# Small tensors of a router moved to PSUM, additions and factors moved to ScalarE, and the last expert's matmuls put in another order

## The chip, the cores and the metric

The kernel runs on one core of one Trainium2 chip. The metric is the device time of one execution in microseconds (us); a smaller one is better. Shown are the median of three runs and one profiled execution.

## The reference

Three stages follow each other. First windowed attention with four sink keys over 4 batches, 8 heads, 768 positions and 64 values per head; then a SoLU layer on 3072 tokens; then a mixture of eight experts, of which each token takes the one with the largest logit.

```python
scores = np.where(is_sink | in_window, q @ k.T / 8, -1e9)
a = np.exp(scores - max); a = a / (sum(a) + 1e-9)          # attention
x = concat_heads(a @ v)                                     # 3072 x 512
h = x @ w_in; e = np.exp(h - max)                           # SoLU layer, 512 -> 1024
solu = h * e / (sum(e) + 1e-9)
ln = (solu - mean) / sqrt(var + 1e-6) * g_ln
x = ln @ w_out                                              # 3072 x 512
logits = x @ w_gate; idx = argmax(logits); gate = softmax(logits)[idx]
out[idx == e] = gate * (relu(x[idx == e] @ w1[e]) @ w2[e])  # eight experts
```

## The kernel before

The attention (a_... functions) goes through 32 units n of two heads and 384 query rows. For one unit, a_scores computes six blocks of scores; each block is masked and scaled on VectorE (L246, L247), exponentiated on ScalarE with its sum (L250), and after the six blocks 1e-9 is added to the six sums (L256), the reciprocal taken (L257), and GpSimd scales the probabilities (L259 pk, L268 psk). a_sinks(u) transposes the sink probabilities of two units on TensorE (L285); a_trans and a_out transpose the others (L299), mask them on GpSimd (L303, L305) and multiply by the values (L315, L321). The first NATP = 5 units multiply fp32 operands directly (L238); later ones use operands split into a high and a low part of type fp32r (L241, L242). a_scores takes a generator mid, which is a_sinks for a pair of units; it is run after the fourth of the six score blocks.

At the same time the weights w_in and w_out are decoded from eight-byte words and split (decode, load_w_in, load_w_out: L367, L368, L369, L381, L382, L416, L417). load_w_out first makes two factors of 128 x 8 from g_ln (g_s L388, g_l L389).

The second stage (m_... functions) takes 24 tiles of 128 tokens: m_in (x by w_in, L472 to L474), m_act (exponential, moments and normalisation; small 128 x 1 columns of the tile sc are combined on VectorE, L487 to L505), m_tr (transposes, L521), m_out (by w_out together with eight logit columns, L543 to L545; then the router on tiles of 128 x 8, L551 to L559), and m_route, which ranks the tile's tokens within their experts by two small matmuls (L570, L571) from the one-hot tile oh and the running count acc, and stores their ids through GpSimd (L579).

The third stage sorts the experts by their counts and runs each with a fixed capacity; f_in is the first matmul of an expert (L868 to L870), f_out the second (L938 to L940). The eighth has one block of 128 rows; for it f_in_rows keeps tokens on the rows (L894 to L896), transposes the result back (L904), and f_out multiplies 512 columns at a time, evicts them (L945) and stores them by an indirect DMA of GpSimd (L946). G.drain() (L1025) is traced between the two for the last expert, behind the last GpSimd split of its weights (L784).

Attention and second stage are interleaved by estimated costs that the generators yield. Over this order the framework places each engine's instructions in a queue of its own with the aid of a planner that simulates times; issue_after(i) says that an instruction comes after i on its engine. Each engine then works through its queue in order, and semaphores join the engines. PSUM has eight banks: three go round under the tag psa, five under psm; the function ps chooses by name.

```python
ATT, MOE, flip = ("s", "tp", "skp", "av", "le"), ("h", "lt", "x2", "wt", "wt2", "rk", "dt", "dh"), [0]
```

Of the kernel before, what the change touches and what calls it, by code (L numbers as in the profile page):

```python
# [8 lines left out]
F32 = mybir.dt.float32  # L9
# [47 lines left out]
def body(ctx, tc, a):  # L57
# [133 lines left out]
    copied = []  # L191
# [31 lines left out]
    def a_scores(n, mid=()):  # L223
# [5 lines left out]
        for i in range(3):  # L229
            for r in range(2):  # L230
# [4 lines left out]
                if n < NATP:  # L235
                    q, k = qk_t[n][r]
                    with tc.issue_after(par_m.ins) if n == 0 else ExitStack():
                        T.matmul(s[:, 0:272], q[rows, qs], k[rows, ks], start=True, stop=True)  # L238
                else:
                    q, ql, k = qk_t[n][r]  # L240
                    T.matmul(s[:, 0:272], q[:, qs], k[:, ks], start=True, stop=False)  # L241
                    T.matmul(s[:, 0:272], ql[:, qs], k[:, ks], start=False, stop=True)  # L242
# [10 lines left out]
            if i == 1:  # L253
                yield from mid
        P = P.rearrange("p r i c -> p (r i) c")
        V.tensor_scalar(out=sm, in0=sm, scalar1=1.0e-9, scalar2=None, op0=ALU.add)  # L256
# [14 lines left out]
    def a_sinks(u):  # L271
# [12 lines left out]
        for i in range(3):  # L284
            T.transpose(t[:, 128 * i:128 * i + 128], psk[:, i].rearrange("p a b c -> p (a b c)"), ident)  # L285
# [99 lines left out]
    def load_w_out(flush=False):  # L385
        sc = SC_OUT * (1.0 if flush else RAW)
        with tc.issue_after(vx[0].ins) if pin[0] else ExitStack():
            V.tensor_scalar(out=g_s, in0=g_sb, scalar1=sc, scalar2=None, op0=ALU.mult)  # L388
            V.tensor_scalar(out=g_l, in0=g_sb, scalar1=1.0 / SC_OUT, scalar2=None, op0=ALU.mult)  # L389
# [45 lines left out]
    acc = const.tile([128, NE], BF16, name="acc")  # L435
    V.memset(acc, 0.0)
    iot8 = const.tile([128, NE], F32, name="iot8")
# [44 lines left out]
    def m_act(t):  # L482
# [10 lines left out]
        V.scalar_tensor_tensor(out=sm, in0=sm, scalar=1.0e-9, in1=sc[:, 3:4], op0=ALU.add, op1=ALU.add)  # L493
        V.scalar_tensor_tensor(out=es, in0=sm, scalar=1.0e-6, in1=sm, op0=ALU.mult, op1=ALU.mult)
# [38 lines left out]
    def m_out(t, row0, mid=()):  # L533
        lh, ll = ln_t.pop(t)
        xr = xrow[t % NXR]
        L = const.tile([128, NE], F32, tag="L", name="L", bufs=2)
        q = const.tile([128, 4], F32, tag="q", name="q", bufs=2)
        oh = const.tile([128, NE], BF16, tag="oh", name="oh", bufs=3)
        for c in range(2):
# [9 lines left out]
            if c == 0:  # L549
                lg = p[:, 256:264]  # L550
# [6 lines left out]
                V.tensor_scalar(out=oh, in0=iot8, scalar1=q[:, 2:3], scalar2=None, op0=ALU.is_equal)  # L557
# [9 lines left out]
    def m_route(t, ids, free=False):  # L567
# [3 lines left out]
        T.matmul(p[:, 0:NE], ones_b, acc, start=False, stop=True)  # L571
        r = const.tile([128, NE], F32, tag="r", name="r")
        s_ = const.tile([128, 1], F32, tag="s_", name="s_", bufs=3)
        si = const.tile([128, 1], I32, tag="si", name="si", bufs=3)
        V.tensor_tensor(out=acc, in0=acc, in1=oh, op=ALU.add)
        V.tensor_tensor(out=r, in0=p[:, 0:NE], in1=rowb, op=ALU.add)  # L576
# [98 lines left out]
    def count():  # L675
        p = ps("ct")
        T.matmul(p[:, 0:NE], ones_b, acc, start=True, stop=True)
        V.tensor_copy(cnt, p[:, 0:NE])

    def plan_head():  # L680

        count()
# [164 lines left out]
    def f_in(r):  # L847
# [5 lines left out]
        if ROOM[r] == 128:  # L853
            yield from f_in_rows(r)
# [601 lines left out]
```

## Time and profile before

| | |
|---|---|
| median of 3 runs | 808.34 us (807.8 to 811.78) |
| profiled execution | 805.58 us, its span 803.6 us |
| TensorE (PE) busy | 774.0 us, 96% of the span, 5005 matmuls |
| VectorE (DVE) busy | 471.9 us, 59%, 1760 instructions |
| ScalarE (ACT) busy | 459.1 us, 57% |
| GpSimd (POOL) busy | 357.9 us, 45% |
| mean granted TensorE clock | 0.983 of full speed |

The span is from the first to the last instruction. Engines work side by side, so the busy shares don't add up; a share over the whole span is a mean over stages with different limits. A busy TensorE isn't one at its peak, because matmuls are pipelined and their ends are modelled.

### The profile page before, as it was taken

How to read it: one execution, taken by the hardware profiler on the slowest of the kernel's cores; microseconds unless marked ns; L12 is line 12 of the kernel's file. 1: busy time of each engine (PE TensorE's matmuls, PEld its weight loads, DVE VectorE, ACT ScalarE, POOL GpSimd, SP SyncE). 2: the span in 40 equal slices, each digit the busy share in tenths (PEclk: the TensorE clock that was granted, in tenths of full speed). 3: DMA queues.
4: the chain of work that ended last, by engine and by line, in shares of the span. 5: the costliest groups of instructions: out<-in, count | busy, mean ns of one | idle time of the engine just before them, and what ended most of it. 6: DMA issues, size and time to landing. Idle time of an engine off the chain costs nothing.

```text
span 803.6 us, 15251 instructions
## 1 busy us (share of the span) xinstructions
PE 774.0 (96%) x5005; PEld 667.1 (83%) x5005; DVE 471.9 (59%) x1760; ACT 459.1 (57%) x1209; POOL 357.9 (45%) x396
## 2 busy tenths in 40 slices
PE   6799999999999999999999999999999999999996
PEld 3487788888888977988888889898978888989885
DVE  6788747668657666667486566436324444545541
ACT  5776857758758657667576464154414343536442
POOL 4955264553635545445623021445326244535543
PEclk9869999999999999999999999999999999999999
DMA  9696354596555855458720271484375517663640
GB/s 333 182 277 161 99 139 140 109 144 141 129 121 136 180 103 146 125 129 115 149 68 14 23 256 42 137 290 150 117 257 184 182 59 214 220 207 101 227 174 29
DMA packets 64218, 120.81 MB, mean 150 GB/s; under 512 B 11068, under 2 KB 32190, under 8 KB 64130
## 3 DMA queue, kind: packets, MB, share of 16 engines
q1 hardware_dynamic: 56594, 97.06, 45.8%
q0 software_dynamic: 5088, 13.88, 4.9%
q10 hardware_dynamic: 2448, 8.80, 3.2%
q8 instruction: 42, 0.69, 0.4%
q14 instruction: 46, 0.38, 0.3%
HBM read 80.61 MB, written 13.28 MB: 117 GB/s over the span
## 4 chain that ended last, share of the span: by engine, by line
PE 79%; DVE 10%; ACT 3%; DMA 3%; issue 3%; POOL 1%; POOLq 0%; SPq 0%; ACTq 0%; DVEq 0%
PE ht L868 6%; PE ht L870 6%; PE ht L869 6%; PE y L938 5%; PE y L940 5%; PE x L543 5%; PE y L939 5%; PE x L545 5%; PE h L472 5%; PE x L544 5%; PE h L473 5%; PE av L321 4%; PE h L474 4%; PE s L241 3%; PE lt L521 2%
## 5 line engine op out<-in xcount | busy, mean ns | idle before, releaser
L543 PE MATMUL x<-woh,lh 128*128 128x256 f32 (+1 forms) x384 | 111.5, 291 | 0.7 <-DVE r L576 0.7
L545 PE MATMUL x<-woh,ll 128*128 128x256 f32 (+1 forms) x384 | 109.6, 286 | 0.0
L544 PE MATMUL x<-wol,lh 128*128 128x256 f32 (+1 forms) x384 | 108.8, 284 | 0.0
L250 ACT ACTIVATE P<-P,mx 128x144 f32<-128x144 f32 x192 | 78.3, 409 | 46.3 <-DVE mx L247 43.7
L776 ACT ACTIVATE wh<-wst 128x1024 fp32r<-128x1024 f32 x64 | 67.4, 1058 | 47.4 <-PE ht L869 27.9
L784 POOL TENSOR_TENSOR wl<-wst,wh 128x1024 fp32r<-128x1024 f32 x28 | 67.7, 2419 | 56.9 <-ACT wh L776 49.7
L204 POOL TENSOR_TENSOR d<-d,A 128x560 fp32r<-128x560 f32 (+1 forms) x27 | 33.8, 1253 | 108.1 <-ACT A L203 98.4
L869 PE MATMUL ht<-xel,wh 128*128 128x288 f32 (+5 forms) x256 | 81.2, 319 | 0.0
L870 PE MATMUL ht<-xeh,wl 128*128 128x288 f32 (+5 forms) x256 | 81.1, 318 | 0.0
L784 DVE TENSOR_TENSOR wl<-wst,wh 128x1024 fp32r<-128x1024 f32 x36 | 54.6, 1524 | 44.8 <-ACT wh L776 44.8
L868 PE MATMUL ht<-xeh,wh 128*128 128x288 f32 (+5 forms) x256 | 79.9, 318 | 0.0
L938 PE MATMUL y<-wh,hh 128*128 128x512 f32 x192 | 77.9, 406 | 1.2 <-DVE hl L877 1.2
L472 PE MATMUL h<-wih,bxh 128*128 128x512 f32 x192 | 78.4, 408 | 0.2
L473 PE MATMUL h<-wil,bxh 128*128 128x512 f32 x192 | 76.3, 397 | 0.0
L940 PE MATMUL y<-wh,hl 128*128 128x512 f32 x192 | 76.0, 397 | 0.0
L939 PE MATMUL y<-wl,hh 128*128 128x512 f32 x192 | 75.8, 395 | 0.0
L474 PE MATMUL h<-wih,bxl 128*128 128x512 f32 x192 | 74.1, 397 | 0.0
L543 PEld LDWEIGHTS x<-woh,lh 128*128 128x128 f32 x384 | 72.3, 188 | 2.2 <-ACT bxh L831 0.9
L545 PEld LDWEIGHTS x<-woh,ll 128*128 128x128 f32 x384 | 72.3, 188 | 1.2 <-issue 0.7
L544 PEld LDWEIGHTS x<-wol,lh 128*128 128x128 f32 x384 | 72.4, 189 | 0.6
L247 DVE CUSTOM_DVE_ANT_0 P<-s,mk 128x144 f32<-128x144 f32 x192 | 55.7, 300 | 20.8 <-PE s L242 11.3
L246 DVE COPY_PREDICATED s<-pick,s 128x128 f32<-128x128 int32 x160 | 44.9, 291 | 38.4 <-PE s L242 34.8
(279 smaller groups left out, 2014.8 us busy)
## 6 DMA issues: line engine op xcount, KB each, us to landing
wst<-w SPq DMA_DIRECT2D x64, 512.0 KB, 4.3
d<-qk SPq DMA_DIRECT2D x15, 472.0 KB, 3.7
x_d<-xrow SPq DMA_DIRECT2D x24, 264.0 KB, 6.4
d<-qk SPq DMA_DIRECT2D x13, 400.0 KB, 3.6
B<-A SPq DMA_DIRECT2D x27, 192.0 KB, 4.0
A<-A SPq DMA_DIRECT2D x27, 192.0 KB, 2.7
B<-A SPq DMA_DIRECT2D x15, 332.0 KB, 5.0
w<-w_in ACTq DMA_DIRECT2D x8, 512.0 KB, 6.6
```

The source lines that it names most:

```text
L472: T.matmul(h, xh[k], wih[:, k, cs], start=(k == 0), stop=False)
L473: T.matmul(h, xh[k], wil[:, k, cs], start=False, stop=False)
L543: T.matmul(p[:, 0:n], lh[:, k, :], woh[:, k, c, 0:n], start=(k == 0), stop=False)
L544: T.matmul(p[:, 0:n], lh[:, k, :], wol[:, k, c, 0:n], start=False, stop=False)
L545: mm = T.matmul(p[:, 0:n], ll[:, k, :], woh[:, k, c, 0:n], start=False, stop=(k == 7))
L784: return (G if c % 2 and r else V).tensor_tensor(out=l_, in0=st_w.pop((r, which, c)), in1=raw(h_), op=ALU.subtract)
L868: T.matmul(o, wh[:, k, fs], xh(k), start=(k == 0), stop=False)
L869: T.matmul(o, wh[:, k, fs], xl(k), start=False, stop=False)
L870: T.matmul(o, wl[:, k, fs], xh(k), start=False, stop=(k == 3))
L938: T.matmul(o, hh[:, k, sl], wh, start=(k == 0), stop=False)
L939: T.matmul(o, hh[:, k, sl], wl, start=False, stop=False)
L940: T.matmul(o, hl[:, k, sl], wh, start=False, stop=(k == 7))
```

## The change

Six places. (1) In a_scores the 1e-9 is added by ScalarE. (2) The factors g_s and g_l are made by ScalarE, placed behind an exponential (pin) in place of a VectorE instruction (vx). (3) In m_act two columns are combined by tensor_scalar with a per-partition operand in place of scalar_tensor_tensor. (4) In m_out the tile L lies in the PSUM bank that holds the logits; oh is compared from L; the running count is a new tile for each token tile (accs), written in m_out; in m_route the tile r lies in PSUM, and the addition to acc is left out there. (5) For the first eight units the sinks' generator runs after all six score blocks, and the first three pairs' transposes are placed behind the latest score matmul. (6) The last expert is one function, f_rows, which takes the 512 output columns in two halves, transposes the first half of the hidden values before the last quarter of them is computed, begins the second matmul with three of its eight row blocks between the two transposes' turns, evicts the two halves one after the other, and issues the store; f_out isn't called for it, and G.drain() is traced behind it.

```diff
@@ -188,7 +188,7 @@
-    copied = []
+    copied, last_s = [], [None]
@@ -235,11 +235,11 @@
                     with tc.issue_after(par_m.ins) if n == 0 else ExitStack():
-                        T.matmul(s[:, 0:272], q[rows, qs], k[rows, ks], start=True, stop=True)
+                        last_s[0] = T.matmul(s[:, 0:272], q[rows, qs], k[rows, ks], start=True, stop=True)
                 else:
...
                     T.matmul(s[:, 0:272], q[:, qs], k[:, ks], start=True, stop=False)
-                    T.matmul(s[:, 0:272], ql[:, qs], k[:, ks], start=False, stop=True)
+                    last_s[0] = T.matmul(s[:, 0:272], ql[:, qs], k[:, ks], start=False, stop=True)
                 cc = slice(3 * r + i, 3 * r + i + 1)
@@ -250,10 +250,10 @@
                 yield 0.45 if n < NATP else 0.23
-            if i == 1:
+            if i == (2 if n < 8 else 1):
                 yield from mid
         P = P.rearrange("p r i c -> p (r i) c")
-        V.tensor_scalar(out=sm, in0=sm, scalar1=1.0e-9, scalar2=None, op0=ALU.add)
+        A.activation(out=sm, in_=sm, func=AF.Copy, bias=1.0e-9)
         V.reciprocal(sm, sm)
@@ -281,8 +281,9 @@
         t = ps("skp")
-        for i in range(3):
-            T.transpose(t[:, 128 * i:128 * i + 128], psk[:, i].rearrange("p a b c -> p (a b c)"), ident)
+        with tc.issue_after(last_s[0].ins) if u < 3 else ExitStack():
+            for i in range(3):
+                T.transpose(t[:, 128 * i:128 * i + 128], psk[:, i].rearrange("p a b c -> p (a b c)"), ident)
         A.activation(out=skt, in_=t[:, 0:384], func=AF.Copy, scale=odd)
@@ -384,9 +385,9 @@
         sc = SC_OUT * (1.0 if flush else RAW)
-        with tc.issue_after(vx[0].ins) if pin[0] else ExitStack():
-            V.tensor_scalar(out=g_s, in0=g_sb, scalar1=sc, scalar2=None, op0=ALU.mult)
-            V.tensor_scalar(out=g_l, in0=g_sb, scalar1=1.0 / SC_OUT, scalar2=None, op0=ALU.mult)
+        with tc.issue_after(pin[0].ins) if pin[0] else ExitStack():
+            A.activation(out=g_s, in_=g_sb, func=AF.Copy, scale=sc)
+            A.activation(out=g_l, in_=g_sb, func=AF.Copy, scale=1.0 / SC_OUT)
@@ -432,8 +433,9 @@
     V.memset(ones_b, 1.0)
-    acc = const.tile([128, NE], BF16, name="acc")
+    acc = const.tile([128, NE], BF16, name="acc0")
     V.memset(acc, 0.0)
+    accs, looped = {0: acc}, [False]
     iot8 = const.tile([128, NE], F32, name="iot8")
@@ -490,8 +492,8 @@
                                    accum_out=sc[:, 4 + c:5 + c])
-        V.scalar_tensor_tensor(out=sm, in0=sm, scalar=1.0e-9, in1=sc[:, 3:4], op0=ALU.add, op1=ALU.add)
-        V.scalar_tensor_tensor(out=es, in0=sm, scalar=1.0e-6, in1=sm, op0=ALU.mult, op1=ALU.mult)
+        V.tensor_scalar(out=sm, in0=sm, scalar1=1.0e-9, scalar2=sc[:, 3:4], op0=ALU.add, op1=ALU.add)
+        V.tensor_scalar(out=es, in0=sm, scalar1=1.0e-6, scalar2=sm, op0=ALU.mult, op1=ALU.mult)
         V.tensor_scalar(out=mu, in0=mu, scalar1=sc[:, 5:6], scalar2=-1.0 / (32 * DF), op0=ALU.add, op1=ALU.mult)
@@ -533,7 +535,6 @@
         xr = xrow[t % NXR]
-        L = const.tile([128, NE], F32, tag="L", name="L", bufs=2)
         q = const.tile([128, 4], F32, tag="q", name="q", bufs=2)
@@ -547,14 +548,18 @@
             if c == 0:
-                lg = p[:, 256:264]
+                lg, L = p[:, 256:264], p[:, 272:272 + NE]
                 V.tensor_reduce(out=q[:, 0:1], in_=lg, axis=AX.X, op=ALU.max)
...
                 V.tensor_reduce(out=q[:, 2:3], in_=L, axis=AX.X, op=ALU.min)
-                V.tensor_scalar(out=oh, in0=iot8, scalar1=q[:, 2:3], scalar2=None, op0=ALU.is_equal)
+                V.tensor_scalar(out=oh, in0=L, scalar1=q[:, 2:3], scalar2=None, op0=ALU.is_equal)
+                if not looped[0]:
+                    accs[t + 1] = const.tile([128, NE], BF16, tag="acc", name="acc", bufs=4)
+                    V.scalar_tensor_tensor(out=accs[t + 1], in0=L, scalar=q[:, 2:3], in1=accs[t], op0=ALU.is_equal,
+                                           op1=ALU.add)
                 V.tensor_scalar(out=q[:, 1:2], in0=q[:, 1:2], scalar1=1.0e-9, scalar2=None, op0=ALU.add)
@@ -568,12 +573,13 @@
         T.matmul(p[:, 0:NE], tri, oh, start=True, stop=False)
-        T.matmul(p[:, 0:NE], ones_b, acc, start=False, stop=True)
-        r = const.tile([128, NE], F32, tag="r", name="r")
+        T.matmul(p[:, 0:NE], ones_b, acc if looped[0] else accs[t], start=False, stop=True)
+        r = p[:, 0:NE]
         s_ = const.tile([128, 1], F32, tag="s_", name="s_", bufs=3)
         si = const.tile([128, 1], I32, tag="si", name="si", bufs=3)
-        V.tensor_tensor(out=acc, in0=acc, in1=oh, op=ALU.add)
-        V.tensor_tensor(out=r, in0=p[:, 0:NE], in1=rowb, op=ALU.add)
+        if looped[0]:
+            V.tensor_tensor(out=acc, in0=acc, in1=oh, op=ALU.add)
+        V.tensor_tensor(out=r, in0=r, in1=rowb, op=ALU.add)
         V.scalar_tensor_tensor(out=r, in0=r, scalar=1.0, in1=oh, op0=ALU.mult, op1=ALU.mult, accum_out=s_)
@@ -672,14 +678,14 @@
-    def count():
+    def count(n=NT):
         p = ps("ct")
-        T.matmul(p[:, 0:NE], ones_b, acc, start=True, stop=True)
+        T.matmul(p[:, 0:NE], ones_b, acc if looped[0] else accs[n], start=True, stop=True)
         V.tensor_copy(cnt, p[:, 0:NE])
...
-        count()
+        count(TE + 1)
         V.scalar_tensor_tensor(out=lead, in0=cnt, scalar=float(NE), in1=e8, op0=ALU.mult, op1=ALU.subtract)
@@ -851,7 +857,7 @@
         if ROOM[r] == 128:
-            yield from f_in_rows(r)
+            yield from f_rows(r)
             return
@@ -879,34 +885,65 @@
-    def f_in_rows(r):
+    def f_rows(r):
         hp = pool2["h"]
...
+        w1, w2 = wt[r]
         hh, hl = ht_t[r]
         (xh, xl, c0, n), = xe_t.pop(r)
...
+        p = [ps("ht") for _ in range(2)]
+        hr = [hp.tile([128, DM], F32, tag="y", name="hr", bufs=3) for _ in range(2)]
+        ys = [ps("y") for _ in range(2)]
+        y = hp.tile([128, DM], F32, tag="y", name="y", bufs=3)
+        j = first[r]
+
+        def rows(c):
+            wh, wl = w1[c]
+            o = p[c // 2][:, 256 * (c % 2):256 * (c % 2) + 256]
+            for k in range(4):
+                T.matmul(o, xh(k), wh[:, k, :], start=(k == 0), stop=False)
+                T.matmul(o, xh(k), wl[:, k, :], start=False, stop=False)
+                T.matmul(o, xl(k), wh[:, k, :], start=False, stop=(k == 3))
+
+        def turn(c):
             t = ps("xt")
             for k in range(4):
...
+                i = T.transpose(t[:, 128 * k:128 * k + 128], hr[c][:, 128 * k:128 * k + 128], ident)
             tv = t.rearrange("p (k n) -> p k n", k=4)
...
             V.tensor_tensor(out=hl[:, sl, 0:128], in0=tv, in1=raw(hh)[:, sl, 0:128], op=ALU.subtract)
...
+            return i
+
+        def columns(d, *ks):
+            ds, o = slice(256 * d, 256 * d + 256), ys[d][:, 0:256]
+            for x, w in ((hh, 0), (hh, 1), (hl, 0)):
+                for k in ks:
+                    i = T.matmul(o, x[:, k, 0:128], w2[k // 2][w][:, k % 2, ds], start=(x is hh and k + w == 0),
+                                 stop=(x is hl and k == 7))
+            return i
+
+        rows(0)
+        yield
+        rows(1)
+        yield
+        A.activation(out=hr[0], in_=p[0], func=AF.Relu)
+        rows(2)
+        yield
+        with tc.issue_after(turn(0).ins):
+            rows(3)
+        yield
+        A.activation(out=hr[1], in_=p[1], func=AF.Relu)
+        with tc.issue_after(columns(0, 0, 1, 2).ins):
+            i = turn(1)
+        with tc.issue_after(i.ins):
+            columns(0, 3)
+            columns(1, 0, 1, 2, 3)
+        for d in range(2):
+            columns(d, 4, 5, 6, 7)
+            A.activation(out=y[:, 256 * d:256 * d + 256], in_=ys[d][:, 0:256], func=AF.Copy, scale=gate[:, j:j + 1])
+        G.indirect_dma_start(out=a["out"], out_offset=bass.IndirectOffsetOnAxis(ap=dst[:, j:j + 1], axis=0), in_=y,
+                             in_offset=None, bounds_check=B * S - 1, oob_is_err=False)
+        yield
@@ -1028,7 +1065,7 @@
                 next(nx, None)
-            for m, _ in enumerate(f_out(r, m0)):
+            for m, _ in enumerate(f_out(r, m0) if more else ()):
                 for _ in range((4 * m + 4) // nm - 4 * m // nm):
@@ -1177,7 +1214,7 @@
             open_moe1(c2, "_g")
-            dec_p[0] = mp
+            dec_p[0], looped[0] = mp, True
             for g in (load_w_in(True), load_w_out(True)):
```

## Rows read from the trace of the kernel before

**Rows 1.** Windows: us, busy (count) of PE, PEld, DVE, ACT, POOL; PE clock; DMA.

```profile
40.00:56.00 16.00, 15.02 (x67) 12.55 (x67) 14.06 (x49) 11.30 (x31) 7.60 (x11) 0.50 0.88 246
56.00:290.00 234.00, 232.28 (x1637) 200.69 (x1637) 161.47 (x701) 164.17 (x491) 118.56 (x139) 1.00 0.61 140
290.00:304.00 14.00, 11.51 (x78) 9.52 (x78) 11.12 (x37) 8.96 (x30) 3.75 (x4) 1.00 0.49 122
304.00:520.00 216.00, 212.42 (x1474) 188.45 (x1474) 138.25 (x630) 128.73 (x375) 78.78 (x95) 1.00 0.45 106
```

**Rows 2.** Timeline of VectorE around 303 us, and TensorE just after it.

```profile
302.05 0.84 DVE L493 SCALAR_TENSOR_TENSOR sc<-sc 128x1 f32<-128x1 f32 x1
...
304.01 0.17 PE L570 MATMUL rk<-oh,tri 128*128 128x8 bf16 x1 [1.21 <-DVE L L552]
```

**Rows 3.** VectorE's groups by shape: busy us, mean ns; idle before, releaser.

```profile
L557 DVE TENSOR_SCALAR oh<-iot,q 128x8 bf16<-128x8 f32 x24 | 10.4, 434 | 0.0
L555 DVE SCALAR_TENSOR_TENSOR L<-L,iot 128x8 f32<-128x8 f32 x24 | 9.5, 395 | 2.1 <-ACT ex L554 2.0
L256 DVE TENSOR_SCALAR sm<-sm 128x6 f32<-128x6 f32 x32 | 8.9, 279 | 8.5 <-ACT P L250 8.4
L493 DVE SCALAR_TENSOR_TENSOR sc<-sc 128x1 f32<-128x1 f32 x24 | 8.7, 362 | 0.0
L494 DVE SCALAR_TENSOR_TENSOR sc<-sc 128x1 f32<-128x1 f32 x24 | 7.4, 308 | 0.0
L575 DVE TENSOR_TENSOR acc<-acc,oh 128x8 bf16<-128x8 bf16 x24 | 6.7, 281 | 10.0 <-PE rk L571 9.6
L552 DVE TENSOR_SCALAR L<-x,q 128x8 f32<-128x8 f32 x24 | 5.3, 221 | 0.1
...
L685 DVE TENSOR_SCALAR lead<-lead,led 128x8 f32<-128x8 f32 x1 | 0.2, 221 | 0.0
```

**Rows 4.** Single lines: duration in ns, minimum/median/maximum, first and last start.

```profile
L493 DVE SCALAR_TENSOR_TENSOR sc<-sc x24: 146/156/1201, 76.4 to 478.0; 128x1 f32<-128x1 f32 x24
L495 DVE TENSOR_SCALAR sc<-sc x24: 198/202/215, 76.6 to 479.5; 128x1 f32<-128x1 f32 x24
```

**Rows 5.** ScalarE's groups by shape, same columns as rows 3.

```profile
L500 ACT ACTIVATE sc<-sc 128x1 f32<-128x1 f32 x24 | 4.7, 199 | 1.2 <-DVE sc L499 1.2
L926 ACT ACTIVATE y<-y,gate 128x256 f32<-128x256 f32 x2 | 1.0, 476 | 5.7 <-PE y L923 5.7
```

**Rows 6.** Timelines of VectorE and GpSimd near 38 us.

```profile
37.98 2.37 DVE L388 TENSOR_SCALAR g_s<-gw_sb 128x8 f32<-128x8 f32 x1
39.47 0.85 POOL L305 TENSOR_SCALAR_AFFINE_SELECT pt<-pt 128x768 f32<-128x768 f32 x1
```

**Rows 7.** Timeline of TensorE, early: start, us, group [idle before, releaser].

```profile
24.60 0.55 PE L285 MATMUL skp<-ident,psk 128*128 128x128 f32 x3 [2.70 <-POOL psk L268]
...
40.37 2.40 PE L321 MATMUL wt<-pt,vd 128*64 128x256 f32 x12 [1.47 <-POOL pt L305]
43.38 1.09 PE L395 MATMUL wt<-ident,dec 128*128 128x128 f32 x4 [0.61 <-DVE dec L369]
```

**Rows 8.** Timeline of the last expert: TensorE, then ScalarE's last eviction.

```profile
783.66 0.36 PE L894 MATMUL ht<-wh,xeh 128*128 128x256 f32 x1
...
789.07 0.28 PE L896 MATMUL ht<-wh,xel 128*128 128x256 f32 x1
...
790.09 0.66 PE L904 MATMUL xt<-ident,hr 128*128 128x128 f32 x4 [0.30 <-ACT hr L899]
790.57 0.50 PE L938 MATMUL y<-wh,hh 128*128 128x512 f32 x1
...
796.30 0.39 PE L940 MATMUL y<-wh,hl 128*128 128x512 f32 x1
...
796.78 0.69 ACT L945 ACTIVATE y<-y,gate 128x512 f32<-128x512 f32 x1 [5.40 <-PE y L940]
```

**Rows 9.** GpSimd's drain, in the columns of rows 4.

```profile
L1025 POOLq DRAIN  x1: 10020/10020/10020, 785.5 to 785.5; - x1
```

More of the change, by code (lines that the diff above doesn't have):

```diff
@@ L880, in f_in @@
         xe_t.pop(r)
-    def f_in_rows(r):
+    def f_rows(r):
         hp = pool2["h"]
-        w1 = wt[r][0]
+        w1, w2 = wt[r]
         hh, hl = ht_t[r]
         (xh, xl, c0, n), = xe_t.pop(r)
-        hr = []
-        for c in range(2):
-            p = ps("ht")
-            for q in range(2):
-                wh, wl = w1[2 * c + q]
-                o = p[:, 256 * q:256 * q + 256]
-                for k in range(4):
-                    T.matmul(o, xh(k), wh[:, k, :], start=(k == 0), stop=False)
-                    T.matmul(o, xh(k), wl[:, k, :], start=False, stop=False)
-                    T.matmul(o, xl(k), wh[:, k, :], start=False, stop=(k == 3))
-                yield
-            h_ = hp.tile([128, DM], F32, tag="y", name="hr", bufs=3)
-            A.activation(out=h_, in_=p, func=AF.Relu)
-            hr.append(h_)
-        for c in range(2):
+        p = [ps("ht") for _ in range(2)]
[11 more added lines that the diff above has]
+        def turn(c):
             t = ps("xt")
             for k in range(4):
-                T.transpose(t[:, 128 * k:128 * k + 128], hr[c][:, 128 * k:128 * k + 128], ident)
+                i = T.transpose(t[:, 128 * k:128 * k + 128], hr[c][:, 128 * k:128 * k + 128], ident)
             tv = t.rearrange("p (k n) -> p k n", k=4)
@@ L908, in f_in_rows @@
             V.tensor_tensor(out=hl[:, sl, 0:128], in0=tv, in1=raw(hh)[:, sl, 0:128], op=ALU.subtract)
-            yield
+            return i
[28 more added lines that the diff above has]
+        yield
     def f_out(r, m0=0, m1=None, late=()):
```

## The prediction

> **What bounds the kernel now.** I read the windows first, then VectorE's groups and the spread of single lines in them, and last the timelines of the two ends with the waits of TensorE. The windows settle most of it: from 56 to 290 us TensorE is busy 232.28 of 234 us, and from 304 to 520 us 212.42 of 216 [rows 1]. The clock is granted at 1.00 in all three of the windows after 56 us, and the diff touches nothing of the expert stage behind 520 us before its last expert. So VectorE, however much of it is freed, can give back only what TensorE stands idle: 1.7 us, 2.5 us and 3.6 us in the three windows between 56 and 520 us, 7.8 us in all. The largest piece is the short one, 290 to 304 us: there VectorE is busy 11.12 of 14 us, and TensorE waits 1.21 us for a router instruction of VectorE (L552) [rows 1, 2]. [...]
>
> **Why VectorE's small instructions are long.** L493 works on one number per partition. Its median is 156 ns, its mean 362 ns and its maximum 1201 ns; L495, which works on the same tile with per-partition operands, stays between 198 and 215 ns [rows 3, 4]. So the first has a cost that comes from beside it. The g_s instruction shows from where: 128x8 numbers take 2.37 us, from 37.98 to 40.35 us, and GpSimd's L305 ends at 40.32 us [rows 6]. It stood until GpSimd was done. The groups of the change are those with two SBUF tensors, or with a wide SBUF tensor as the only one; L552, which reads PSUM, shows a mean of 221 ns over 24 and is not stretched [rows 3].
>
> **The change, part by part.**
>
> *Router, moments, 1e-9.* I give each changed form the price of the nearest form that isn't stretched [rows 3, 4]. L557 and L555 at L552's 5.3 us for 24: 10.4 and 9.5 fall by 5.1 and 4.2. L575 goes, and a similar instruction on L takes its place: 6.7 to 5.3, 1.4 saved. L493 and L494 at 24 x 0.202 = 4.8 us: 3.9 and 2.6 saved. L256 leaves VectorE: 8.9. With g_s, 2.4: 28.5 us of VectorE's time. ScalarE gets 32 + 2 instructions at L500's 0.199 us [rows 5], 6.8 us; they lie beside TensorE's work unless a unit waits for them (a rival below).
>
> What this is worth on the path: in 290 to 304 us two tiles pass, with two L493 and two L494 of the kind of which one stands in rows 2; that one would be 0.84 - 0.20 = 0.64 us shorter, four of them about 2.5 us, which is the whole idle time of the window (2.49). Other work of VectorE in that stretch stays, and TensorE will be late for something else, so I take two thirds, 1.6 us. In the other two windows the 5.3 us of idle time is spread over waits on several engines; I take a ninth, 0.6 us. The bounds are 0 and 7.8. What comes to be late next is VectorE's long unaltered work, as the mask blocks and moments. Sum here: -2.2.
>
> The matmul that ranks tokens (L570, L571) still has VectorE's wait behind it: today L575 waits for it, 9.6 us in total [rows 3]; then the addition that makes r does, with the same work queued behind it. I count nothing, neither gain nor loss. The banks of logits and ranks are held longer by about the length of five instructions of 0.22 us, 1.1 us; five banks go round and a tile takes seven in turn, so that a bank is asked for again after most of a tile's matmuls, and this lies beside them. Without that cover each tile would lose those 1.1 us.
>
> [...] L552 reads PSUM and L685 does a comparison of the same shape from SBUF, and both show 221 ns [rows 3], so by the rows the place is free. [...]
>
> *g_s and g_l.* VectorE stands 2.37 us at 37.98 us. Behind it are the sums of unit 3, score blocks of unit 4, and the dec for which TensorE waits 0.61 us at 43.38 [rows 6, 7]. All 0.61 should go. More can't be had directly: before it TensorE waits for GpSimd, which this doesn't hasten.
>
> *Sinks' transposes.* At 24.60 us TensorE stands 2.70 us in front of L285 with two score matmuls of the same unit behind it in the queue [rows 7]. These now go ahead. But TensorE waits for GpSimd again at 40.37, after 1.47 us of idleness, and GpSimd's work up to there is the same; most of the gain is given back there. In unit 4 the last two blocks can also come before the transposes, and perhaps into the 1.47 us. I take 0.4 us, so the early part is -1.0; the bounds are a loss of 1.5 (the transposes too late for a following product) and a gain of 0.61 + 1.47 + 2.70 = 4.8.
>
> *Last expert.* 48 matmuls of 256 columns start between 783.66 and 789.07, 0.115 us apart. The second matmul becomes 48 of these instead of 24 of 512 columns. The transposes' turns take 790.57 - 790.09 = 0.48 us each. The new end: 783.66 + 96 x 0.115 + 2 x 0.48 = 795.66; plus 0.28 - 0.115 for the last one's pipeline, 795.83; plus the 0.09 us that lie between the last matmul and its eviction now (796.30 + 0.39 to 796.78), plus 0.48 for an eviction of 256 columns [rows 5, 8]: 796.40. Today it is 796.78 + 0.69 = 797.47. Gain 1.1 us; the waits between are covered, because about ten matmuls (1 us) lie between each transpose and its use. The drain ends at 785.5 + 10.0 = 795.5 [rows 9], 0.9 us before the store wants to go, so it limits the gain to 1.9. Bounds 0 and 1.9.
>
> **Sum.** -2.2 - 1.0 - 1.1 = -4.3 us: the profiled execution of 805.58 (span 803.6, 2.0 around it) becomes 801.3. The median of the runs is 2.8 above it, so the predicted median is 808.34 - 4.3 = 804.0.
>
> **Rivals.** *Freed time off the path* (0.27): VectorE's stretched instructions lie mostly beside TensorE's work, which is busy 99% of 56 to 520 us; the planner's new order makes about as many waits as it removes. Only the tail stays, with at most 1 us beside it: 807.2 to 806. For it: 5.3 of the 7.8 us aren't tied to the changed lines. Against: the wait at 304.01.
>
> [...]
>
> *The drain behind the store* (0.07): it is now traced after it. If it also stands after it in GpSimd's queue, part of its 10.0 us [rows 9] shows at the end; its wait for the weights' split doesn't, so I take half: 804.0 + 5 = 809. Against: it is ready long before the store, and the planner goes by readiness.
>
> *ScalarE late with the sums* (0.08), the one that makes it slower: the 1e-9 now stands in ScalarE's queue, and the reciprocal at the head of VectorE's queue waits for it, with the mask blocks behind. If the planner lets one of ScalarE's long instructions in between, each of 32 units loses some 0.4 to 0.7 us of VectorE. Were half of this on TensorE's path, 32 x 0.28 = 9 us, the time would be 813. It decides from (4.3 + 4.0) / 32 = 0.26 us per unit. Against: VectorE waited 8.4 us here for the exponentials already [rows 3], so the instruction only joins a wait that exists.
>
> **How the numbers follow.** My forecast has 0.48: some of TensorE's waits go, 799.5 to 806, likeliest 804.0. A measurement of this kernel can't tell less than about 0.5%, 4.0 us, from no change; that border is 804.3, close to the forecast, so its chance is divided nearly in two. Faster: 0.33 of the forecast, 0.10 of the clock and 0.02 of the rest, 0.45. Slower: 0.08, with 0.01 of the drain, 0.09. Same: 0.46. The range leaves out the slow ends of the last two rivals and the best of the clock: 799.8 to 808.2.
>
> **What would show it.** Right: L493, L494, L555 and L557 have maxima near 220 ns; the window of 290 to 304 us, or what answers to it, has over 13 us of TensorE; no g_s on VectorE; L285's first wait is gone, and the wait for dec too; the last eviction ends 12.7 us after the last expert's first matmul. Wrong: TensorE waits for a reciprocal or for ScalarE's sum; the granted clock is 0.50 beyond 56 us; a drain of GpSimd stands behind the last store.

## The result, and the profile after

The kernel after the change takes 813.07 us (median of 6 runs, 809.09 to 815.26), the kernel before beside it 807.8: a ratio of 1.0074, 95% interval [1.005, 1.0098]. It is slower by 0.7%, some 6 us. The forecast was 804.0, with a range of 799.8 to 808.2 and a chance of 0.09 for slower. The profiled execution after took 815.26 us (span 813.5), the one of before 805.58; it is the longest of its six, so that the 9.7 us between the two overstate the 6 us of the ratio.

The windows of the trace after, same columns as [rows 1], with one more at 180 us:

```profile
40.00:56.00 16.00, 11.55 (x59) 9.51 (x59) 13.61 (x37) 9.80 (x28) 6.69 (x8) 0.72 0.80 203
56.00:290.00 234.00, 226.59 (x1577) 197.38 (x1576) 144.15 (x665) 159.79 (x492) 112.78 (x132) 0.98 0.63 136
290.00:304.00 14.00, 14.00 (x96) 12.15 (x95) 5.97 (x27) 6.76 (x21) 6.13 (x7) 1.00 0.50 119
304.00:520.00 216.00, 211.37 (x1489) 188.56 (x1487) 134.96 (x632) 135.12 (x404) 79.23 (x93) 0.99 0.47 104
...
180.00:200.00 20.00, 15.07 (x86) 12.76 (x84) 9.71 (x36) 6.67 (x20) 2.81 (x4) 0.83 0.51 111
```

The stretch of 14 us that had 2.49 us of idle TensorE has none now. But 56 to 290 us has lost 5.7 us of busy time and 60 matmuls; 4.9 us of idleness lie in the 20 us from 180 to 200, and 54 of those matmuls are missing there. Before, the same 20 us read:

```profile
180.00:200.00 20.00, 19.71 (x140) 17.38 (x139) 17.27 (x79) 15.41 (x47) 6.84 (x8) 1.00 0.66 139
```

The chain that ended last, after, around that place (start us, us, what), and TensorE's waits in the same trace (in total, times, longest):

```profile
163.10 1.39 POOL d L204
164.49 0.98 POOL A L205
...
166.00 8.28 DMA B<-A
...
174.30 10.63 DMA A<-A
...
185.07 0.57 PE s L241
```

```profile
PE s L241 <- DMA A<-A: 4.8, 2, 4.3
...
PE skp L286 <- DVE mx L247: 2.5, 1, 2.5
...
PE skp L286 <- DMA w<-w_in: 1.8, 1, 1.8
```

L204 and L205 split the operands of an attention unit, and L209 copies parts of them (the tiles A and B) to the other 64 partitions with DMAs of which one has to land before the next may overwrite what it read. One copy took 8.28 us and the next 10.63; TensorE stood 4.3 us in front of the unit's first scores (L241). Then its clock fell:

```profile
180.00:184.00 4.00, 0.81 (x10) 0.42 (x6) 0.58 (x1) 0.49 (x1) 1.27 (x2) 0.93 0.77 44
184.00:190.00 6.00, 4.93 (x16) 4.29 (x17) 2.10 (x8) 1.39 (x5) 0.00 (x0) 0.50 0.55 169
```

After 4 us with 0.81 us of matmuls, 0.50 was granted, as before had it from 40 to 56 us. Matmuls of 512 columns start 0.43 us apart there (L474 to L476, 188.25 to 189.53 us), and 0.23 us in the trace of before at 1.00 (L472 to L474, 182.45 to 184.77 us); so 4.93 us at 0.50 do, by an estimate from these, the work of 2.6. The two together make most of the difference of 9.7 us between the profiled executions: 19.71 - 15.07 = 4.6 us of busy time less, and the 2.3 us lost to the clock. Elsewhere the clock went both ways: 1.00 from 26 to 32 us and 0.72 from 40 to 56 us were granted where before had 0.50, but in two later stretches 0.72 where before had 1.00, in the second behind two waits of 0.7 and 1.3 us:

```profile
70.00:76.00 6.00, 5.92 (x26) 5.23 (x27) 4.08 (x19) 4.03 (x13) 2.04 (x2) 0.72 0.53 141
312.00:318.00 6.00, 4.82 (x28) 4.73 (x29) 5.06 (x36) 6.00 (x26) 3.76 (x5) 0.72 0.69 163
```

The instructions that the change aimed at have lost their long executions. Single lines after, columns of [rows 4]: the two moments, the router's masked index, oh and the count that replaces the addition of before, and then the page's totals:

```profile
L495 DVE TENSOR_SCALAR sc<-sc x24: 206/208/211, 79.4 to 487.8; 128x1 f32<-128x1 f32 x24
L496 DVE TENSOR_SCALAR sc<-sc x24: 201/204/211, 80.2 to 489.4; 128x1 f32<-128x1 f32 x24
L556 DVE SCALAR_TENSOR_TENSOR x<-x,iot x24: 157/174/175, 102.9 to 506.6; 128x8 f32<-128x8 f32 x24
L558 DVE TENSOR_SCALAR oh<-x,q x24: 212/226/228, 103.3 to 507.0; 128x8 bf16<-128x8 f32 x24
L561 DVE SCALAR_TENSOR_TENSOR acc<-x,q,acc x24: 213/218/221, 103.5 to 507.1; 128x8 bf16<-128x8 f32 x24
```

```profile
PE 778.9 (96%) x5029; PEld 674.4 (83%) x5029; DVE 452.5 (56%) x1726; ACT 461.2 (57%) x1244; POOL 362.5 (45%) x396
```

Early, TensorE still stops at the sinks' transposes, and at a second pair of them 21 us later. At the end come the last expert's first matmul, its two evictions one right behind the other, and GpSimd's drain:

```profile
24.73 0.90 PE L286 MATMUL skp<-ident,psk 128*128 128x128 f32 x3 [1.81 <-DMA w<-w_in]
...
41.90 1.30 PE L322 MATMUL wt<-pt,vd 128*64 128x256 f32 x12 [0.78 <-POOL pt L306]
45.68 0.52 PE L286 MATMUL skp<-ident,psk 128*128 128x128 f32 x3 [2.48 <-DVE mx L247]
...
793.46 0.36 PE L903 MATMUL ht<-wh,xeh 128*128 128x256 f32 x1
...
805.79 0.84 ACT L943 ACTIVATE y<-y,gate 128x256 f32<-128x256 f32 x2 [3.88 <-PE y L921]
```

```profile
L1062 POOLq DRAIN  x1: 9978/9978/9978, 795.3 to 795.3; - x1
```

### The profile page after: what moved, and what is told of

The parts are those of the page before. It is cut to its first block, busy times and chain, and to the rows that moved or that the text cites. A ratio compares the mean times of both kernels' runs of the same rounds, so it can differ in the third digit from the quotient of the medians.

```text
span 813.5 us, 15246 instructions
## 1 busy us (share of the span) xinstructions
PE 778.9 (96%) x5029; PEld 674.4 (83%) x5029; DVE 452.5 (56%) x1726; ACT 461.2 (57%) x1244; POOL 362.5 (45%) x396
## 4 chain that ended last, share of the span: by engine, by line
PE 78%; DMA 10%; DVE 4%; issue 3%; ACT 2%; POOL 2%; POOLq 0%; SPq 0%; ACTq 0%; DVEq 0%
PE ht L874 6%; PE ht L876 6%; PE ht L875 6%; PE x L544 5%; PE h L474 5%; PE y L975 5%; PE y L977 5%; PE h L475 5%; PE x L546 5%; PE y L976 5%; PE x L545 5%; PE h L476 5%; PE av L322 4%; DMA B<-A 3%; PE s L241 2%
## 5 line engine op out<-in xcount | busy, mean ns | idle before, releaser
L544 PE MATMUL x<-woh,lh 128*128 128x264 f32 (+1 forms) x384 | 111.5, 290 | 0.1
L546 PE MATMUL x<-woh,ll 128*128 128x264 f32 (+1 forms) x384 | 109.8, 286 | 0.0
L545 PE MATMUL x<-wol,lh 128*128 128x264 f32 (+1 forms) x384 | 109.1, 284 | 0.0
L790 POOL TENSOR_TENSOR wl<-wst,wh 128x1024 fp32r<-128x1024 f32 x28 | 68.8, 2457 | 50.5 <-ACT wh L782 43.2
L204 POOL TENSOR_TENSOR d<-d,A 128x560 fp32r<-128x560 f32 (+1 forms) x27 | 33.8, 1253 | 121.9 <-ACT A L203 95.7
L790 DVE TENSOR_TENSOR wl<-wst,wh 128x1024 fp32r<-128x1024 f32 x36 | 57.9, 1618 | 45.7 <-ACT wh L782 43.8
L474 PE MATMUL h<-wih,bxh 128*128 128x512 f32 x192 | 78.9, 412 | 0.1
L975 PE MATMUL y<-wh,hh 128*128 128x512 f32 x184 | 74.9, 407 | 1.2 <-DVE hl L883 1.2
L476 PE MATMUL h<-wih,bxl 128*128 128x512 f32 x192 | 75.5, 402 | 0.0
L976 PE MATMUL y<-wl,hh 128*128 128x512 f32 x184 | 72.9, 396 | 0.0
L977 PE MATMUL y<-wh,hl 128*128 128x512 f32 x184 | 72.8, 398 | 0.0
L247 DVE CUSTOM_DVE_ANT_0 P<-s,mk 128x144 f32<-128x144 f32 x192 | 56.2, 302 | 21.4 <-PE s L242 15.9
```

What stands on the lines that cost most here:

```text
L474: T.matmul(h, xh[k], wih[:, k, cs], start=(k == 0), stop=False)
L476: T.matmul(h, xl[k], wih[:, k, cs], start=False, stop=(k == 3))
L544: T.matmul(p[:, 0:n], lh[:, k, :], woh[:, k, c, 0:n], start=(k == 0), stop=False)
L545: T.matmul(p[:, 0:n], lh[:, k, :], wol[:, k, c, 0:n], start=False, stop=False)
L546: mm = T.matmul(p[:, 0:n], ll[:, k, :], woh[:, k, c, 0:n], start=False, stop=(k == 7))
L790: return (G if c % 2 and r else V).tensor_tensor(out=l_, in0=st_w.pop((r, which, c)), in1=raw(h_), op=ALU.subtract)
```

## The experiments

Each ratio is to the kernel before, run beside it on the same chip. The last column counts, over the instructions that both programs have, how many of TensorE's some 4,600 stand at another place in its queue than in the kernel before; one that moves ahead counts for all that it passes.

| run | ratio | interval | moved on TensorE |
|---|---|---|---|
| change as a whole | 1.0074 | 1.005 to 1.0098 | 2282 |
| last expert alone | 1.0003 | 0.9984 to 1.0022 | 0 |
| router and moments alone | 1.0001 | 0.9979 to 1.0023 | 1607 |
| additions on ScalarE alone | 1.0114 | 1.0082 to 1.0147 | 1361 |
| sinks and factors | 1.0049 | 1.0033 to 1.0066 | 881 |
| sinks alone | 1.0027 | 1.0014 to 1.004 | 881 |
| factors alone | 1.003 | 1.0007 to 1.0053 | 21 |
| additions left out, nothing else | 0.9974 | 0.995 to 0.9999 | 95 |
| change, additions left out | 0.9927 | 0.9909 to 0.9945 | 1449 |

### One part of the change at a time

Theory A was that the loss comes with a new order, in which the copies of the operands are late; B blamed the router's chain, C the reciprocal's wait for ScalarE's sum.

**Last expert alone** (the diff's f_rows and the call of it, nothing else).

> The kernel before with the last expert's function of the change alone (f_rows); the order of everything ahead of the last experts is that of before. From the trace after the change, where the stretch from the last expert's first matmul to its last eviction takes 13.2 us (13.8 before): both theories expect 0.6 us less than before, ratio 0.998 to 1.000. If the loss sits in the last expert (its store, the drain) the kernel would be 3 us or more slower.

1.0003 [0.9984, 1.0022]. From 789.47 to the end of two evictions at 801.39 + 0.88 the stretch takes 12.80 us, where [rows 8] make 13.81: a gain of 1.0 us that the ratio doesn't resolve. The loss isn't here.

**Router and moments alone** (L, r, oh, accs and the two tensor_scalar).

> The kernel before with the router's tiles in PSUM, the separate counts and the two tensor_scalar in the moments alone. Theory A (the loss of 5 us is a late copy of the operands near 185 us, which another part of the change brings about): 2 us less to no change, ratio 0.997 to 1.001. Theory B (the router's chain itself holds TensorE or the banks): 3 to 6 us more, ratio 1.004 to 1.008, with waits of TensorE for r or for a bank of the second stage.

1.0001. B falls, and the forecast 2.2 us didn't come either; the order changed at 1607 places. The window that the forecast was built on did gain 1.8 us (13.33 busy, 11.51 before), but the one ahead of it lost 2.3 (230.02, 232.28 before):

```profile
56.00:290.00 234.00, 230.02 (x1626) 198.88 (x1626) 153.00 (x694) 162.85 (x487) 117.99 (x139) 1.00 0.62 138
290.00:304.00 14.00, 13.33 (x91) 11.24 (x90) 10.48 (x43) 8.32 (x27) 2.80 (x4) 1.00 0.58 129
```

**Additions on ScalarE alone.**

```diff
-        V.tensor_scalar(out=sm, in0=sm, scalar1=1.0e-9, scalar2=None, op0=ALU.add)
+        A.activation(out=sm, in_=sm, func=AF.Copy, bias=1.0e-9)
```

> The kernel before with the addition of 1e-9 on ScalarE alone. Theory A: no direct cost, 1 us less to 1 us more, ratio 0.998 to 1.002. Theory C (the prediction's rival: the reciprocal waits for ScalarE's sum and VectorE's queue with it): 3 us or more slower, ratio above 1.004, with VectorE's wait in front of the reciprocal grown by 0.26 us or more a unit.

1.0114, nine us slower, the worst of the parts. It looked like C. But the trace has TensorE's wait for copies of A, in all 6.8 us, and the window from 180 us is as empty as after the change:

```profile
PE s L241 <- DMA A<-A: 6.8, 3, 3.6
```

```profile
180.00:200.00 20.00, 15.06 (x92) 12.69 (x92) 11.02 (x38) 7.96 (x26) 4.65 (x7) 0.91 0.53 135
```

**Sinks and factors.**

> The kernel before with the early part alone: the sinks' transposes behind the sixth block's scores for the first eight units, and the factors g_s and g_l on ScalarE. Theory A (this part shifts the early units against the second stage, and the operands' copies come late near 185 us): 4 to 8 us slower, ratio 1.005 to 1.010, with a wait of TensorE for the copies of 3 us or more and the clock falling behind it. Theories B and C: 1 us less to no change, ratio 0.998 to 1.000.

1.0049, 4 us slower as A had it, but TensorE waits for no copy of A in its trace: the place that A named was wrong here. The waits grew at VectorE's masked scores, from 5.2 us in 3 to 8.3 us in 5; that this is what costs the 4 us is not shown:

```profile
PE s L238 <- DVE mx L247: 8.3, 5, 2.4
```

### Instructions and order taken apart

Four kernels hold every engine's queue in the order of another kernel, by an edge from each instruction to the one that stood ahead of it there (an edge for the order, not a wait):

```diff
-    moe2()
+    moe2(); hold_order(tc)
...
+        for p, n in zip(ns, ns[1:]):
+            tc.add_manual_dep(at[n], p, mybir.DependencyInfo(mybir.DependencyClass.NoSync, mybir.DependencyReason.DATA), reason='order')
```

VectorE's custom instructions (L247) and late weight loads can't be held in this way; they fall between their neighbours.

**Additions on ScalarE, order of before.**

> The 1e-9 on ScalarE, but every engine's instructions held in the order of the kernel before; the 32 additions stand on ScalarE directly behind the last exponential of their unit. Theory C (the reciprocal's wait for ScalarE's sum costs the 9 us that the addition cost alone): 7 us or more slower, ratio 1.008 to 1.015. Theory A (the cost is the new order that the planner dealt, with the second stage ahead of the attention and the operands' copies late): ratio 0.997 to 1.003.

0.9996 [0.998, 1.0011]. C falls: the 32 instructions cost nothing that can be told where the order stays, though VectorE stands longer in front of the reciprocals for ScalarE's sum (8.2 us in 9 waits) than in the run of the additions alone (5.1 in 7):

```profile
  ACT sm L256: 8.2, 9
```

**Instructions of before, order of the run with the additions alone.**

> The instructions of the kernel before, the 1e-9 on VectorE directly ahead of the reciprocal, but every engine in the order that the planner dealt when the addition alone was on ScalarE. Theory C: as before, ratio 0.998 to 1.002. Theory A: the loss stays without the edit, ratio 1.008 to 1.015, with TensorE's wait for the operands' copies near 185 us.

1.0188 [1.0157, 1.0219], above A's range too. The loss stays without the edit, and is larger:

```profile
PE s L241 <- DMA A<-A: 9.4, 3, 4.1
```

**All instruction changes, order of before.**

> All instruction changes (router in PSUM, moments, 1e-9 and factors on ScalarE, last expert) with every engine held in the order of the kernel before; the sinks' transposes stay where they were, and the new function of the last expert is ordered by the planner. Theory A: the instructions themselves give 0 to 4 us, ratio 0.994 to 1.000. Theory C: the sum's wait stays, ratio 1.004 or more.

0.9987 [0.9959, 1.0015]: no loss, and no gain that can be told from none.

**Instructions of before, order of after.**

> The instructions of the kernel before, the last expert's included, but every engine held in the order of the kernel after the change; the sinks' transposes of three pairs, the factors' and the last expert's places are the planner's. Theory A: as slow as after the change or slower, ratio 1.005 to 1.012. Theory C: ratio 0.998 to 1.003.

1.0168 [1.0141, 1.0195], above A's range as well. With the instructions of before, the order of after costs 13.6 us (0.0168 of 808), and TensorE waits for copies again:

```profile
PE s L241 <- DMA A<-A: 6.7, 2, 3.5
```

With the instructions of after it costs 7.6 us less (1.0074). In the order of before, those instructions, the sinks' edit left out, gave 1 us that can't be told from none. The 7.6 us aren't shown to be the instructions' own: the sinks' transposes of three pairs, the factors, the last expert and L247 aren't held in place, both reversed kernels run instructions in an order that was dealt for others, and no run tells what the holding itself costs there.

### Why the copies are late

In the trace after, GpSimd issued a store of token ids (L585) at 173.43 us, and it took 11.3 us to land; of the copies issued beside it, the two whose landing the trace has took 10.2 and 10.6 us. (The copy of 8.28 us above set out at 166.00, ahead of that store, when the store before, issued at 157.8, landed after 8.2 us; what made it slow is not shown.) Theory D was that the store makes them late, E that they would be waited for anyway. Two runs left out the first 21 id stores, each held in one of the two orders; all experts then gather row 0, so that what the stores cost is read from the two runs against each other, and a gain against the kernel before can hold something of the experts too.

```diff
-        i = G.indirect_dma_start(out=id_d, out_offset=bass.IndirectOffsetOnAxis(ap=si[:, 0:1], axis=0),
+        i = free and G.indirect_dma_start(out=id_d, out_offset=bass.IndirectOffsetOnAxis(ap=si[:, 0:1], axis=0),
                                  in_=ids, in_offset=None)
```

> The kernel after the change, every engine held in its order, with the stores of token ids left out for the first 21 tiles (the ids stay zero, so the experts of this run all gather row 0). Theory D (the copies of the operands are late near 185 us because an id store of some 10 us is under way beside them): the copies land in 3 to 6 us, TensorE's wait for them there is gone, 4 to 8 us less than the kernel after, ratio to before 0.997 to 1.003. Theory E (the order has put the attention's chain late, and the copies would be waited for whatever runs beside them): the wait of 3 us or more stays, ratio 1.005 to 1.010.

> The control of the run without id stores: the kernel before in its own order, with the same stores left out. Both theories: 0 to 2 us less than before, ratio 0.997 to 1.001; what it gives is to be taken off the other run's gain.

0.9978 [0.9956, 1.0] in the order of after, 0.9935 [0.9912, 0.9958] in that of before. What L209's copies took to land (minimum, median, maximum), first in the trace after from 172 to 187 us, then in the run without stores, in the order of after, from 164 to 187 us, and its window:

```profile
  PE s L241: 4.3, 1
...
DMA to landing us min/median/max: 10.2/10.4/10.6
```

```profile
DMA to landing us min/median/max: 2.3/2.9/3.5
```

```profile
180.00:200.00 20.00, 18.65 (x128) 16.04 (x127) 15.38 (x76) 14.47 (x52) 6.10 (x8) 1.00 0.48 121
```

D is right about the place: without the store the copies land in 3 us, the wait is gone and the clock stays at 1.00. In time it is right in part. The order of after gains 1.0074 - 0.9978, 7.8 us, but the control gains 5.3, more than both theories had for it. Of the 6.0 us between the two kernels 0.0043 (3.5 us) remain between the two orders, and neither theory explains them.

Over all the runs, the four traces in which TensorE waits 4.8 us or more for copies of A belong to the four slowest kernels (4.8, 6.8, 6.7 and 9.4 us at 1.0074, 1.0114, 1.0168 and 1.0188); the sinks with the factors lose their 4 us without such a wait.

### Which edit, and a version that is faster

**Additions left out, nothing else.** A sum holds the exponential of the maximum, so it is at least 1, and 1e-9 doesn't change it in fp32.

```diff
-        V.tensor_scalar(out=sm, in0=sm, scalar1=1.0e-9, scalar2=None, op0=ALU.add)
+
```

> The kernel before with the 32 additions of 1e-9 left out altogether (each sum is at least 1, so that fp32 doesn't change by it), the order left to the planner. Theory A (any edit makes the planner deal the order anew, and the deal is worth more than the instruction): 3 us or more away from before on either side, ratio below 0.996 or above 1.004, though nothing was added. If the time follows the work: 0 to 1 us less, ratio 0.998 to 1.000.

0.9974: 2 us less, the border of what can be told. TensorE's order hardly moved (95), so A's "any edit" was too strong.

**All instruction changes in the order of before, additions left out, last expert's halves in turn.**

```diff
-            columns(1, 0, 1, 2, 3)
+            i = columns(1, 0, 1, 2, 3)
         for d in range(2):
-            columns(d, 4, 5, 6, 7)
+            with tc.issue_after(i.ins): i = columns(d, 4, 5, 6, 7)
```

> All instruction changes held in the order of the kernel before, the additions of 1e-9 left out altogether, and the last expert's second half of columns held behind its first half, so that the first eviction lies beside matmuls. Theory A: faster than both kernels, 1 to 4 us less than before, ratio 0.995 to 0.999; the stretch from the last expert's first matmul to its last eviction 12.5 to 12.8 us.

0.9989 [0.9961, 1.0017], not told from no change. The edit of the tail does what it was meant to, the first eviction now lies beside matmuls, but it brings nothing: the stretch is 794.99 + 0.47 - 782.52 = 12.94 us, above the forecast and no shorter than the 12.80 us of the last expert alone, where both evictions come at the end.

```profile
793.62 0.47 ACT L942 ACTIVATE y<-y,gate 128x256 f32<-128x256 f32 x1 [2.66 <-PE y L920]
794.99 0.47 ACT L942 ACTIVATE y<-y,gate 128x256 f32<-128x256 f32 x1 [0.90 <-PE y L920]
```

**Sinks alone, factors alone** (the diff's lines 253 and 284, and 387 to 389).

> The kernel before with the sinks' edit alone (transposes behind the sixth block's scores in the first eight units). Theory A (this edit makes the planner deal the order anew, and that costs the 4 us of the early part): ratio 1.003 to 1.007. Theory F (the factors on ScalarE cost it): ratio 0.998 to 1.001, and TensorE's first wait for the sinks' product gone.

> The kernel before with the factors g_s and g_l on ScalarE alone; the planner leaves nearly all of the order as it was. Theory A: 0 to 1 us less, ratio 0.998 to 1.001, and TensorE's wait for dec shorter. Theory F: ratio 1.003 to 1.007.

1.0027 [1.0014, 1.004] and 1.003 [1.0007, 1.0053]; F falls for the sinks, A for the factors. The twelve times of the factors alone spread from 807.5 to 816.3 us; the profiled execution, 814.6, shows a wait for a copy that the kernel before doesn't have:

```profile
PE s L241 <- DMA A<-A: 2.5, 1, 2.5
```

That this copy is just in time in the shorter executions is possible, and not shown.

**The change without the additions; additions left out with the last expert alone.**

> The kernel after the change with the additions of 1e-9 left out altogether (the sums don't change by it), the order left to the planner. Theory A (the additions on ScalarE brought the order with the late copies): TensorE's wait for the copies near 185 us is gone or under 1 us, ratio 0.999 to 1.004. Theory G (the loss of the change is the sinks' own, the additions are cover): ratio 1.004 to 1.009.

> The kernel before without the additions of 1e-9 and with the last expert's new function, its second half of columns held behind the first half; nothing else of the change. 2 us less by the additions and 1 us less at the end, the stretch from the last expert's first matmul to its last eviction 12.8 us or less: ratio 0.994 to 0.998. If the run without the additions was only lucky, 0.998 to 1.001.

0.9927 [0.9909, 0.9945], 803.73 us, which beats both kernels: by the ratios 5.9 us below before and 11.9 below after, and below what either theory had. Its trace has no wait for a copy of A. The second is 0.9972 [0.9958, 0.9986]; its last expert takes 12.79 us.

**The change as it is, in the order of the run just told; additions back on VectorE, order free.**

> All instructions of the kernel after the change, the additions on ScalarE included and placed directly behind the last exponential of their unit, but every engine held in the order that the planner dealt when the additions were left out. Theory A (the order is all): within 1.5 us of the kernel after without additions, ratio 0.991 to 0.996. Theory C (the additions on ScalarE cost time themselves): ratio 1.000 or more.

> The kernel after the change with the additions of 1e-9 back on VectorE, the order left to the planner, which deals one more. Theory A: no wait of TensorE for copies near 185 us unless this order is again of the late kind; ratio 0.993 to 1.002, its place in it not foreseen. Theory C: ratio 0.993 to 0.996, as without the additions, since only the harmful part is gone.

0.9957 [0.9934, 0.998] and 0.9977 [0.9956, 0.9998]. The first has the instructions of the kernel after, ScalarE's additions included. Its window at 180 us, against 15.07 at 0.83 after:

```profile
180.00:200.00 20.00, 20.00 (x140) 17.61 (x138) 14.95 (x71) 14.95 (x48) 6.86 (x8) 1.00 0.69 135
```

From 1.0074 to 0.9957, 9.5 us, by order alone. That the run without additions is a little faster still (0.9927) lies at the edge of both intervals. The second run's order is a third one, and its time too; it lies above C's range.

## Why the prediction was wrong

**The step that failed** is a term that the sum put at nothing: the order of the queues. The text ahead says that a planner which simulates times places every queue, and the sum of -2.2, -1.0 and -1.1 us has no term for what it deals anew; only one rival mentions a new order, as making "about as many waits as it removes". Measured, the order moves the same instructions from 0.9957 to 1.0074, 9.5 us, and those of before up to 1.0188. Against that a sum of 4.3 us can't be read. What the prediction says of the additions themselves, "they lie beside TensorE's work unless a unit waits for them", holds (0.9996 in the order of before). How the order costs its time is shown in part: copies that come late beside an id store (10.2 to 10.6 us) make TensorE wait (4.3 us) and its clock fall (0.50), and without the stores the difference of the two kernels is 3.5 us instead of 6.0; what those 3.5 us are stays open.

**The slower rivals** had the wrong mechanism. The reciprocal does wait for ScalarE's sum, but that costs nothing that can be told by itself. The drain, 795.3 + 9.98 = 805.3 us, ends ahead of the store at 806.90. The sign that came true was on the list without a rival of its own: a clock of 0.50 beyond 56 us, behind a wait for a DMA that the rows of before don't show as late.

**VectorE's prices were right.** The maxima are 175 to 228 ns. The five lines above take 24.7 us (24 times their medians), where those that they replace, the additions and g_s took 54.0 [rows 3, 6]: 29.3 us, forecast 28.5. The engine's total fell by 19.4 alone, because others became longer (L784's 54.6 us are L790's 57.9 after, L417's 7.3 are L418's 9.5). The prediction's cause, that VectorE stood until GpSimd was done, fits the place of [rows 2]: there L493 and L494 end at 302.89 and 303.81 us, and GpSimd's L303 and L305 at 302.87 and 303.80:

```profile
303.00 0.81 DVE L494 SCALAR_TENSOR_TENSOR sc<-sc 128x1 f32<-128x1 f32 x1
...
302.01 0.86 POOL L303 TENSOR_SCALAR_AFFINE_SELECT pt<-pt 128x768 f32<-128x768 f32 x1 [1.13 <-ACT pt L300]
302.94 0.86 POOL L305 TENSOR_SCALAR_AFFINE_SELECT pt<-pt 128x768 f32<-128x768 f32 x1
```

L493, with a tensor operand, took up to 1201 ns, and L495 after, without one, at most 211; no run takes GpSimd's part in this by itself. PSUM cost next to nothing: L556, which reads and writes it, took 174 ns at the median, and the same instruction on SBUF, L555 before, 168:

```profile
L555 DVE SCALAR_TENSOR_TENSOR L<-L,iot x24: 155/168/1491, 106.3 to 496.2; 128x8 f32<-128x8 f32 x24
```

**What they are worth was not.** Forecast were 2.2 us, with two thirds of the 2.49 us in 290 to 304 us. That window did fill, to 14.00 of 14 after the change and by 1.8 us with the router alone, but that run gave nothing (1.0001): TensorE lost 2.3 us ahead of the window, as in the rival of freed time off the path, whose new order makes about as many waits as it removes. The two thirds of one window were a price for the window and not for the kernel.

**Early part.** The wait for dec (0.61 us) is gone from the list of waits after. The first wait of the sinks only fell from 2.70 to 1.81 us. Their gain was given back not at GpSimd's pt, where the wait fell from 1.47 to 0.78, but at the sinks themselves: the next pair's transposes, now behind the last scores too, wait 2.48 us at 45.68. With the factors it is 4 us slower where 1.0 faster was forecast, outside its bounds. The 0.10 that the chances give to TensorE's clock was the author's estimate: in the trace after, 0.72 was granted from 40 to 56 us where before had 0.50, and the kernel came out at 1.0074.

**Last expert.** 13.2 us after the change and 12.8 alone, forecast 12.7, before 13.8. The planner mixed the halves' matmuls, so that both evictions come at the end (0.84 us for two), but that isn't what is missing: with the halves in turn the stretch took 12.94 and 12.79 us. Alone it is as forecast; what lengthens it to 13.2 after the change is not shown.

**Where the size fits, it is luck.** In the order of the run without additions the change's instructions give 3.5 us, near the forecast 4.3, and 5.9 without the additions. But in the order of before they give 1.0 us, not told from none, so the 3.5 us hold what that order gave, and no run shows the sum of 4.3 us as the worth of the instructions.

## What to carry to other kernels

Where a planner places the queues, an edit has two effects, its instructions and the order dealt anew, and the second can be the larger: hold the old order with the new instructions, and the new order with the old ones, before you judge either. In the trace of a kernel whose TensorE is full, look for the transfer chain that is just in time (here two copies in series for each unit, and an id store beside them); it has no idle time in front of it and so appears in no list of waits until an order makes it late.

## What the runs showed of the hardware

An indirect store of 128 ids of four bytes took 7.0 us to landing at the median of the trace after. Near 175 us copies of L209 took 10.2 to 10.6 us beside one, and 2.3 to 3.5 us in the run without the stores, in the same order. Over a whole run, the longest copy fell from 10.1 to 5.5 us in the order of before when 21 such stores were left out, and from 10.6 to 8.6 us in that of after; in the order of before the time fell by 5.3 us, in a kernel whose experts all gather row 0. In the trace after, the copy issued at 174.30 us landed at 184.93, the store beside it at 173.43 + 11.3 = 184.7, within 0.2 us; whether one landing waited for the other or both were merely slow, no run here tells.

In the trace after, TensorE's clock fell to 0.50 behind a wait of 4.3 us, and stood there from 184 to 190 us while the engine was busy 4.93 of 6 us; by the estimate above the clock added 2.3 us to this wait. It fell again at 313 us, behind two waits of 0.7 and 1.3 us, and stood at 0.50 from 314 to 316 us.
